# Batch ends of a cross-covariance attention and gated FFN kernel: wide norms, an inverse in four pieces, and two PSUM banks for the folded weights

One Trainium2 chip, one core. The metric is the device time of one execution in microseconds (us). Inputs are random; q, k, v are 4 x 6016 x 256.

## What is computed

```python
qn = q / (norm(q, axis=1) + 1e-6)            # columns of q and k scaled to length 1, per batch
kn = k / (norm(k, axis=1) + 1e-6)
s = kn.transpose(0, 2, 1) @ qn / tau         # 256 x 256 per batch, tau = 1
a = softmax(s, axis=-1)
x = (v @ a).reshape(24064, 256)
gate = 1 / (1 + exp(-(x @ w_gate)))          # w_gate, w_val: 256 x 1536
out = (gate * (x @ w_val)) @ w_out           # w_out: 1536 x 256
```

## The kernel before

PSUM is the memory that TensorE's matmuls write to; a buffer of a PSUM pool is called a bank here. hT is the gated hidden layer, transposed. The softmax matrix is folded into the weights once per batch: G = a @ w_gate and H = a @ w_val, each 256 x 1536. Then v goes straight through G and H. A batch is 12 chunks of 512 tokens (the last has 384), and each chunk is 12 slots, one per 128 columns of the hidden layer. Work for the next batch (its scores, its norms, its softmax, its G and H) is hung into the slots as side work. So three times in a run, at the end of batches 0, 1 and 2, the next batch's attention matrix is finished between the matmuls of the current one. The first batch's is made in a prologue.

```python
psg = pool("psg", 2, space=PSUM)   # gate products
psv = pool("psv", 2, space=PSUM)   # val products
pso = pool("pso", 2, space=PSUM)   # output products
pss = pool("pss", 1, space=PSUM)   # scores of the next batch
psm = pool("psm", 1, space=PSUM)   # norms, row sums, G/H products
# ... 8 buffers in all

def glu(b, ci, f):                 # one slot
    # 2 matmuls into ps_gate, 2 into ps_val (512 columns each)
    nc.scalar.activation(out=g_sb[:, :n], in_=ps_gate[:, :n], func=ACT.Sigmoid)
    nc.vector.tensor_tensor(out=hT[:, f, :n], in0=ps_val[:, :n], in1=g_sb[:, :n], op=ALU.mult)

def norms_mm(b):                   # chunk 9, slot 10: squared norms as one column per 128 channels
    s["n"] = psm.tile([P, 2 * CB], FP32, tag="m", name="ps_n")
    norm_mms(s["n"], s["acc"], TPC, True, True)      # 16 products of one column

def spread_k(b):                   # chunk 10, slot 2: k's inverse norms along the free axis, in fp32
    s["rk"] = pso.tile([P, C], FP32, tag="o", name="ps_rk")
    # ... matmuls of the column, broadcast, with the fp32 identity

# side work of the next batch n at the end of a batch
at(9 * FC + 10, norms_mm, n)
at(9 * FC + 11, norms_sqrt, n)     # ScalarE: a table load, the root, a table load back
at(10 * FC + 1, norms_inv, n)      # VectorE: + 1e-6, reciprocal of 128 x 4
at(10 * FC + 2, spread_k, n)
# ... copy the scores out of PSUM (slot 1), scale them (slot 4), exp (slot 11)
at(11 * FC + 0, sums, n)           # row sums of exp, in psm
for i in range(len(gh_order)):     # 12 G/H pieces, each 2 matmuls of 512 in psm, then an eviction
    at(11 * FC + i, gh, n, i)

# the main loop: in chunks 9 and 10 the output products of the chunk before are not spread
# over the slots, but come as a block of 4 x 12 after slot 11
block = b + 1 < B and ci in (9, 10)
# ...
if prev is not None and block:
    for s in range(TPC):
        out_mms(*prev, s * FC, (s + 1) * FC)   # 12 matmuls into a pso buffer
        flush()                                # VectorE copies it out
```

## Time and profile before

The median was 842.0 us over three runs.

| engine | busy us | share of 837.4 |
|---|---|---|
| TensorE | 816.6 | 98% |
| VectorE | 565.3 | 68% |
| ScalarE | 389.3 | 46% |

Three views carry the argument: TensorE's timeline around a batch end, ScalarE's and VectorE's there, and the groups of instructions by shape. The prediction shows their lines. One reading habit is used all through: on a pipelined TensorE the distance between *starts* says what an instruction cost, and its duration does not. A pair of 512-column matmuls is listed with 0.59, but the next pair starts 0.43 after it. A start that comes later than this is a wait, whether the bracket at the end of the line names one or not. For VectorE it is the same on a smaller scale: an operation of 0.69 lets the next start after 0.61.

This gives four numbers per batch end, each a difference of two starts: the norms (first norm product to the next gate product), the block of output products of chunk 9, chunk 10 (its first gate product to its first output product) and chunk 11 (its first gate product to the first of the next batch). Before, they are 0.40, 5.24, 11.71 and 19.44 us, and the whole from the first norm product to the next batch takes 42.89, the same to 0.01 at all three ends.

### The profile page before, as it was taken

The numbers are of one execution on the slowest core, as the hardware profiler recorded it, in microseconds if no ns is written. First come the engines' busy times: TensorE is split into PE (matmuls) and PEld (weight loads), VectorE is DVE, ScalarE is ACT, GpSimd is POOL, SyncE is SP. The second block draws the span as 40 slices with busy tenths as digits, with TensorE's granted clock in tenths as the row PEclk, the third lists the DMA queues.
The fourth block names the chain that finished last, engine by engine and source line by source line (L and its number), as shares of the span: only waits on it lengthen the run. The fifth ranks groups of instructions, "written<-read, shape, count | busy, mean of one in ns | idle before, by whom it ended". The sixth has DMA issues, their size and how long they took to land.

```text
span 837.4 us, 13986 instructions
## 1 busy us (share of the span) xinstructions
PE 816.6 (98%) x5327; PEld 506.3 (60%) x5338; DVE 565.3 (68%) x976; ACT 389.3 (46%) x639; POOL 83.9 (10%) x161
## 2 busy tenths in 40 slices
PE   5899999999999999999999999999999999999998
PEld 4546666665666666665566666666566565656666
DVE  2477777776667777777656777777766666666664
ACT  3554444446544444444554444444654444444442
POOL 5532100002011100000210020000000000000000
PEclk9899999999999999999999999999999999999999
DMA  9999624227655543223864353223222522322211
GB/s 176 206 206 188 131 51 89 61 51 142 119 102 107 101 108 63 48 51 89 150 136 86 88 117 78 51 76 67 58 48 51 95 51 76 76 48 68 48 35 69
DMA packets 78738, 76.65 MB, mean 92 GB/s; under 512 B 50768, under 2 KB 55632, under 8 KB 78672
## 3 DMA queue, kind: packets, MB, share of 16 engines
q0 software_dynamic: 24208, 39.33, 28.4%
q1 hardware_dynamic: 54464, 36.45, 15.8%
q8 instruction: 41, 0.67, 0.3%
q14 instruction: 25, 0.20, 0.1%
HBM read 78.64 MB, written 24.64 MB: 123 GB/s over the span
## 4 chain that ended last, share of the span: by engine, by line
PE 91%; DMA 3%; DVE 2%; ACT 1%; issue 1%; POOL 0%; ACTq 0%; POOLq 0%
PE ps_o L88 29%; PE ps_gate L88 28%; PE ps_val L88 28%; PE ps_s L88 4%; DMA k_sb<-in_k_dram 3%; PE ps_gh L88 2%; DVE hT L344 1%; ACT g_sb L343 1%; PE ps_rk L88 0%; ACT gh_H L299 0%; DVE out_sb L370 0%; PE ps_n L88 0%; DVE gh_G L301 0%; DVE gh_H L301 0%; DVE x_sb L246 0%
## 5 line engine op out<-in xcount | busy, mean ns | idle before, releaser
L344 DVE TENSOR_TENSOR hT<-ps_val,g_sb 128x512 bf16<-128x512 f32 (+1 forms) x576 | 390.9, 679 | 220.1 <-ACT g_sb L343 216.2
L343 ACT ACTIVATE g_sb<-ps_gate 128x512 bf16<-128x512 f32 (+1 forms) x576 | 338.6, 588 | 400.0 <-PE ps_gate L88 387.6
L88 PE MATMUL ps_val<-vT,gh_H 128*128 128x512 bf16 (+1 forms) x1152 | 338.1, 375 | 0.5
L88 PE MATMUL ps_gate<-vT,gh_G 128*128 128x512 bf16 (+1 forms) x1152 | 337.5, 375 | 0.5
L88 PE MATMUL ps_o<-w_out_sb,hT 128*128 128x256 bf16 x2256 | 326.1, 273 | 0.0
L88 PEld LDWEIGHTS <-hT 128*128 128x128 bf16 x2256 | 220.7, 98 | 124.8
L88 PEld LDWEIGHTS <-gh_H 128*128 128x128 bf16 x1152 | 112.7, 98 | 132.9 <-ACT gh_H L299 1.5
L88 PEld LDWEIGHTS <-gh_G 128*128 128x128 bf16 x1152 | 112.4, 98 | 37.3 <-ACT gh_G L299 0.3
L370 DVE COPY out_sb<-ps_o 128x256 f32<-128x256 f32 x188 | 78.0, 415 | 20.9 <-PE ps_o L88 20.9
L106 POOL DMA_DIRECT2D v_sb<-in_v_dram x48 | 25.5, 531 | 631.3 <-DMA vT<-v_sb 496.3
L88 PE MATMUL ps_s<-k_sb,q_sb 128*128 128x256 bf16 x376 | 72.3, 295 | 12.2 <-DMA k_sb<-in_k_dram 12.2
L88 PEld LDWEIGHTS <-q_sb 128*128 128x128 bf16 x376 | 39.1, 104 | 20.3 <-issue 7.5
L162 DVE TENSOR_TENSOR sq<-q_sb 128x1024 bf16<-128x1024 bf16 (+3 forms) x46 | 30.4, 661 | 25.3 <-PE ps_n L88 19.1
L200 DVE TENSOR_TENSOR acc<-acc,sq 128x1024 bf16<-128x1024 bf16 (+1 forms) x66 | 44.1, 669 | 0.0
L97 POOL DMA_DIRECT2D k_sb<-in_k_dram x49 | 26.9, 549 | 14.5 <-DMA k_sb<-in_k_dram 9.1
L97 POOL DMA_DIRECT2D q_sb<-in_q_dram x49 | 26.8, 548 | 13.7 <-DMA q_sb<-in_q_dram 6.3
L162 DVE TENSOR_TENSOR sq<-k_sb 128x1024 bf16<-128x1024 bf16 (+2 forms) x34 | 22.4, 658 | 0.0
L160 ACT ACTIVATE sq<-k_sb 128x1024 bf16<-128x1024 bf16 (+1 forms) x12 | 12.2, 1021 | 20.1 <-DMA k_sb<-in_k_dram 19.7
L88 PE MATMUL ps_gh<-w_gate,e_sb 128*128 128x512 bf16 x41 | 12.8, 378 | 1.6 <-DVE rrow L274 1.2
L88 PEld LDWEIGHTS <-e_sb 128*128 128x128 bf16 x112 | 9.9, 97 | 6.8 <-issue 3.2
L88 PE MATMUL ps_gh<-w_val,e_sb 128*128 128x512 bf16 x44 | 13.2, 379 | 0.4
L299 ACT ACTIVATE gh_G<-ps_gh,rrow 128x512 bf16<-128x512 f32 x12 | 8.2, 687 | 9.7 <-PE ps_gh L88 5.6
(44 smaller groups left out, 99.7 us busy)
## 6 DMA issues: line engine op xcount, KB each, us to landing
out_dram<-out_sb SPq DMA_DIRECT2D x44, 512.0 KB, 2.9
q_sb<-in_q_dram POOLq DMA_DIRECT2D x44, 256.0 KB, 6.7
k_sb<-in_k_dram POOLq DMA_DIRECT2D x44, 256.0 KB, 7.6
v_sb<-in_v_dram POOLq DMA_DIRECT2D x44, 256.0 KB, 3.9
out_dram<-out_sb SPq DMA_DIRECT2D x4, 384.0 KB, 2.4
w_gate<-in_moe_w_gate_dram POOLq DMA_DIRECT2D x3, 256.0 KB, 7.0
w_val<-in_moe_w_val_dram POOLq DMA_DIRECT2D x3, 256.0 KB, 7.6
w_out_sb<-in_moe_w_out_dram POOLq DMA_DIRECT2D x1, 768.0 KB, 13.0
```

Source lines behind the costliest of these rows:

```text
L88: nc.tensor.matmul(out, lhsT=lhsT, rhs=rhs, start=start, stop=stop, **kw)
L97: nc.gpsimd.dma_start(out=tl[:, :nt, :], in_=rows(src, b)[:, t0 : t0 + nt, :])
L106: nc.gpsimd.dma_start(out=v_sb[:, :nt, :], in_=rows(v, b)[:, t0 : t0 + nt, :])
L160: nc.scalar.activation(out=sq[:, :nt, :], in_=src[:, :nt, :], func=ACT.Square)
L162: engine.tensor_tensor(out=sq[:, :nt, :], in0=src[:, :nt, :], in1=src[:, :nt, :], op=ALU.mult)
L200: nc.vector.tensor_tensor(out=acc[:, :nt, :], in0=acc[:, :nt, :], in1=st[b]["sq", w][:, :nt, :], op=ALU.add)
L299: nc.scalar.activation(out=dst, in_=ps, func=ACT.Copy, scale=r)
L343: nc.scalar.activation(out=g_sb[:, :n], in_=ps_gate[:, :n], func=ACT.Sigmoid)
L344: nc.vector.tensor_tensor(out=hts[b, ci][:, f, :n], in0=ps_val[:, :n], in1=g_sb[:, :n], op=ALU.mult)
L370: nc.vector.tensor_copy(out=out_sb[:, s, :], in_=ps)
```

## The change

The intent: fewer and better placed waits at the batch ends. k's squared norms come out of TensorE already spread over all partitions (a sum over rows by a matrix of ones, 256 columns: the wide norms), so the fp32 spreading falls away. ScalarE takes the root of 256 columns, and VectorE inverts them in four pieces of 64 in four slots. q's norms stay one column per 128 channels, inverted in slot 1. The scores are scaled straight from PSUM, without the copy. The row sums keep slot 0 of chunk 11, the G/H products start one slot later, and they alternate between the bank of the scores, free by then, and the bank of the norms.

```diff
     def norms_mm(b):
-        s["n"] = psm.tile([P, 2 * CB], FP32, tag="m", name="ps_n")
-        norm_mms(s["n"], s["acc"], TPC, True, True)
+        acc_q, acc_k = s["acc"]
+        s["n"] = psm.tile([P, CB], FP32, tag="m", name="ps_n")
+        s["nk"] = pso.tile([P, C], FP32, tag="o", name="ps_nk")
+        for u in range(TPC):
+            mm(s["nk"], ones_bf, acc_k[:, u, :], u == 0, u == TPC - 1)
+        norm_mms(s["n"], (acc_q,), TPC, True, True)
+
+    def wide_sqrt(b):
+        ...
+        nc.scalar.activation(out=s["rk"], in_=s["nk"], func=ACT.Sqrt)
+        nc.scalar.activation(out=s["r"], in_=s["n"], func=ACT.Sqrt)
+
+    def wide_inv(b, piece):
+        ...
+        cols = ds(piece * (C // 4), C // 4)
+        r = s["rk"][:, cols]
+        nc.vector.tensor_scalar(out=r, in0=r, scalar1=1e-6, scalar2=None, op0=ALU.add)
+        nc.vector.reciprocal(r, r)
+
+    def wide_scale(b, j):
+        nc.vector.tensor_tensor(out=s["x"][:, j, :], in0=s["s"][:, j, :], in1=s["rk"], op=ALU.mult)
 ...
-        at(9 * FC + 11, norms_sqrt, n)
+        at(9 * FC + 11, wide_sqrt, n)
         at(10 * FC + 1, norms_inv, n)
-        at(10 * FC + 2, spread_k, n)
+        for i in range(4):
+            at(10 * FC + 2 + i, wide_inv, n, i)
         for j in range(CB):
-            at(10 * FC + 1, copy_s, n, j)
-        at(10 * FC + 4, scale_k, n)
+            at(10 * FC + 6 + j, wide_scale, n, j)
 ...
         for i in range(len(gh_order)):
-            at(11 * FC + i, gh, n, i)
+            at(11 * FC + min(i + 1, FC - 1), gh, n, i, *((pss, "s"), (psm, "m"))[i % 2])
```

More of the change, by code (lines that the diff above doesn't have):

```diff
@@ L205, in norms_mm @@
         s = st[b]
-        s["n"] = psm.tile([P, 2 * CB], FP32, tag="m", name="ps_n")
-        norm_mms(s["n"], s["acc"], TPC, True, True)
+        acc_q, acc_k = s["acc"]
[5 more added lines that the diff above has]
+    def wide_sqrt(b):
+        s = st[b]
+        s["r"] = attp.tile([P, CB], FP32, tag="rq", name="rq")
+        s["rk"] = attp.tile([P, C], FP32, tag="rk", name="rk")
+        nc.scalar.activation(out=s["rk"], in_=s["nk"], func=ACT.Sqrt)
+        nc.scalar.activation(out=s["r"], in_=s["n"], func=ACT.Sqrt)
+    def wide_inv(b, piece):
+        s = st[b]
+        if piece == 0:
+            s["x"] = attp.tile([P, CB, C], FP32, tag="x", name="x_sb")
+        cols = ds(piece * (C // 4), C // 4)
[3 more added lines that the diff above has]
+    def wide_scale(b, j):
+        s = st[b]
+        nc.vector.tensor_tensor(
+            out=s["x"][:, j, :], in0=s["s"][:, j, :], in1=s["rk"], op=ALU.mult
+        )
     def norms_sqrt(b):
```

## The prediction

> **What bounds the kernel now.** I read the page first (engine shares), then TensorE's timeline around the first batch end, then ScalarE's and VectorE's there, then the groups by shape.
>
> The page says TensorE is nearly always busy:
>
> ```profile
> PE 816.6 (98%) x5327; PEld 506.3 (60%) x5338; DVE 565.3 (68%) x976; ACT 389.3 (46%) x639; POOL 83.9 (10%) x161
> ```
>
> A 98% busy TensorE does not say that it never waits, as matmul ends are modelled and overlap. Its timeline shows the waits as gaps between starts. Columns: start, duration, engine, line, operation, count, idle before.
>
> ```profile
> 199.83 0.54 PE L88 MATMUL ps_n<-ones_bf,acc 128*128 128x1 bf16 x16
> 200.23 0.59 PE L88 MATMUL ps_gate<-vT,gh_G 128*128 128x512 bf16 x2
> ...
> 201.09 5.40 PE L88 MATMUL ps_o<-w_out_sb,hT 128*128 128x256 bf16 x48
> 206.33 0.59 PE L88 MATMUL ps_gate<-vT,gh_G 128*128 128x512 bf16 x2
> ...
> 208.49 0.60 PE L88 MATMUL ps_val<-vT,gh_H 128*128 128x512 bf16 x2
> 209.49 0.71 PE L88 MATMUL ps_rk<-ident_f,r 128*128 128x128 f32 x4 [0.41 <-DVE r L217]
> 210.03 0.59 PE L88 MATMUL ps_gate<-vT,gh_G 128*128 128x512 bf16 x2
> ...
> 213.49 0.59 PE L88 MATMUL ps_gate<-vT,gh_G 128*128 128x512 bf16 x2
> 214.16 0.59 PE L88 MATMUL ps_val<-vT,gh_H 128*128 128x512 bf16 x2
> ```
>
> Two matmuls of 512 start every 0.433 us, so a slot of chunks 9 and 10, one gate and one val product, takes 0.866. The 48 output products take 206.33 - 201.09 = 5.24, or 0.109 each. Between 208.49 and 209.49 there is 0.57 too much (0.433 expected); the spreading of k's norms then costs 210.03 - 209.49 = 0.54; the val product at 214.16 is 0.24 late. Together 1.35 us in chunk 10.
>
> Chunk 11, where the G/H products are made:
>
> ```profile
> 224.37 0.24 PE L88 MATMUL ps_r<-ones_bf,e_sb 128*128 128x1 bf16 x4
> 225.01 0.38 PE L88 MATMUL ps_gh<-w_gate,e_sb 128*128 128x512 bf16 x1 [0.40 <-DVE rrow L274]
> ...
> 230.64 0.60 PE L88 MATMUL ps_o<-w_out_sb,hT 128*128 128x256 bf16 x4
> 231.37 0.59 PE L88 MATMUL ps_gh<-w_gate,e_sb 128*128 128x512 bf16 x2
> ```
>
> Four row sums need about 0.10, so the first G/H product is 0.54 late; it waits for the reading of the row sums out of the one bank that both use. The one at 231.37 is 0.29 late (four 0.109 products end at 231.08), and the one at 240.77 the same. The typical slot is 1.52. Sum 1.12.
>
> So one batch end loses 2.47 us to waits and spreading, three of them 7.4 us, 0.9% of the time. This is a ceiling for the gain; batch 0's norms are made in the prologue, which the change leaves alone. The rest is matmul streaming that is not touched.
>
> **What the Trainium skill says.** "TensorE: Matmul & The Clock Gate", section "Back-to-back issue gap": N/2.4 + 2.5 ns for a warm matmul and a floor of about 25 ns for the smallest. The trace agrees: 109 ns at 256, and 16 one-column products in 200.23 - 199.83 = 0.40, or 25 ns each.
>
> "ScalarE: Activation LUTs", section "What ACT_TABLE_LOAD costs": about 1283 ns for a load, 0.833 ns per element for an activation plus a fixed part. The trace has 1283 ns for the loads and, for sigmoid, 597 ns at 512 and 487 ns at 384, or 0.86 ns per element.
>
> "VectorE: DVE Perf Modes", section "Walkthrough: the 8-slice pipeline in each mode", says that Reciprocal is an iterative divide with a repeat count of 8. I read it as some 8 cycles per element, 8.3 ns at that page's 0.96 GHz. The trace has it only at two tiny sizes, in the groups by shape (busy us, mean ns, idle):
>
> ```profile
> L217 DVE RECIPROCAL r<-r 128x4 f32<-128x4 f32 x4 | 0.7, 178 | 0.1
> L275 DVE RECIPROCAL rrow<-rrow 128x2 f32<-128x2 f32 x4 | 0.7, 166 | 0.1
> ```
>
> Two more elements cost 12 ns, so 6 ns each. It is not a streaming one nanosecond, but two points so near together are a weak measure, and this is the number on which the prediction hangs.
>
> **The change, chunk by chunk, per batch end.**
>
> Chunk 9, norms. Removed: 8 one-column products for k, 8 x 0.025 = 0.20. Added: 4 products of 256, 4 x 0.109 = 0.44. Net +0.24.
>
> Chunk 9, a new wait. The wide norms lie in one of the two buffers of the output pool. The first output product of the block takes the other buffer, and the second takes this one; the built program has a wait for ScalarE in front of that second group. ScalarE frees it only after slot 11's sigmoid, a table load and the wide square root:
>
> ```profile
> 200.86 0.60 ACT L343 ACTIVATE g_sb<-ps_gate 128x512 bf16<-128x512 f32 x1 [0.67 <-PE ps_gate L88]
> 201.47 1.28 ACT L212 ACT_TABLE_LOAD   x1
> 202.77 0.17 ACT L212 ACTIVATE r<-ps_n 128x4 f32<-128x4 f32 x1
> ```
>
> Before, nobody waited for that root at once. Now all moves by 0.24, so the root starts at 203.01 and takes 0.17 + 252 x 0.85 ns = 0.385 (estimate from these rows); with 0.06 to TensorE the second group may start at 203.46. It would be due at 201.33 + 12 x 0.109 = 202.64. New wait: +0.82.
>
> Chunk 10, removed: the wait for the inverse, the fp32 spreading, the late val: -1.35. Two PSUM copies of the scores and two scalings become two scalings straight from PSUM. Added on VectorE: four pieces of add and reciprocal over 64 columns. What VectorE's beat leaves for them:
>
> ```profile
> 208.45 0.69 DVE L344 TENSOR_TENSOR hT<-ps_val,g_sb 128x512 bf16<-128x512 f32 x1 [0.17 <-ACT g_sb L343]
> 209.06 0.16 DVE L216 TENSOR_SCALAR r<-r 128x4 f32<-128x4 f32 x1
> 209.25 0.18 DVE L217 RECIPROCAL r<-r 128x4 f32<-128x4 f32 x1
> 209.35 0.72 DVE L240 COPY x_sb<-ps_s 128x256 f32<-128x256 f32 x2
> ```
>
> The next independent operation starts 0.08 to 0.10 before the last one's end, so one hT product occupies 0.61 of the slot's 0.866: 0.25 is free. A piece is an add, 0.22 until the dependent reciprocal may start, and a reciprocal of 0.166 + 62 x 6 ns = 0.54, less 0.08 overlap: 0.68. It overruns the free time by 0.43, four times: 1.70. The small inverse in slot 1 overruns by 0.03, the two scalings (0.33 each) by 0.08 each. VectorE falls behind by 1.89. TensorE feels this soon: there are two val buffers, and val of slot f+2 needs hT of slot f. In the steady beat that hT ends 1.95 us after its slot's start and the val product is due at 2.17; less the passing-on, 0.17 to 0.18 is forgiven. Stall: 1.89 - 0.18 = 1.71. At 8.3 ns per element a piece takes 0.82 and the stall is 2.29; at 1 ns it takes 0.37 and the stall is 0.5. Net in chunk 10: +0.36, +0.94 or -0.85.
>
> Chunk 11: one slot later the row sums' inverse is long ready (-0.54), and with two banks the products no longer wait for the eviction one slot earlier (-0.58): -1.12. Two products share the last slot, on different banks and different evicting engines, and the scores' bank is asked for only 1.3 us after the last product in it has streamed; with the 0.69 eviction done by then, no new wait.
>
> Sum per batch end: 0.24 + 0.82 + 0.36 - 1.12 = +0.30 at 6 ns, +0.88 at 8.3 ns, -0.91 at 1 ns; three times: +0.9, +2.6, -2.7 us.
>
> **The rivals.** (a) The intended gain: no new wait in chunk 9, pieces that fit the slot: 3 x (0.24 - 1.35 - 1.12) = -6.7, 835 us. Against it: the wait stands in the built program, and the root's start is bound by the table load. (b) A gain in chunk 11 with cheap reciprocals: -2.7, about 839; for it, that 12 ns between two sizes may be a coarse clock tick and not a slope; against it, the page and that somebody found it worth cutting the inverse into four. (c) VectorE becomes the bound of chunk 10 and the pieces only spread its overrun: +0.9 to +2.6, 843 to 845. The 0.25 us of room per slot speaks for it. (d) ScalarE or the late VectorE delays the start of the next stage: hardly, the 5.24 us block of output products after each of chunks 9 and 10 lets both catch up.
>
> **Range and chances.** I weigh 6 ns and 8 ns at about 0.4 each and 1 ns at 0.2; the mean is +0.9, and I lean a little to the iterative divide: +1.2 us, 843.2. An error of a fifth of a us in one wait is 0.6 in the whole. Range 839.0 to 845.8. A fall by 2% is 17 us, more than twice the ceiling; a rise by 2% would need 5.6 us more per batch end. So within 2% almost surely: 0.98, and 0.01 on each side.
>
> **What would show it right or wrong.** In the changed kernel's TensorE timeline: the wide norms and small norms take 0.64 rather than 0.40; an idle of some 0.8 before the thirteenth output product of chunk 9's block, released by the square root; no spreading in chunk 10, but val products each about 0.4 late from slot 5 to slot 8; regular 1.52 us slots in chunk 11. The 64-column reciprocal should show 0.54 to 0.68 us. The prediction is wrong if that reciprocal takes about 0.23, if the buffer of the wide norms is not the one that stalls, or if slower VectorE work, hidden so far, appears in the next batch's first chunk.

## The result and the profile after

The changed kernel took 840.88 us (median of 6 runs, 839.51 to 841.5) beside 841.4 before (6 runs, 839.72 to 842.13). The ratio is 0.9995, with a 95% interval from 0.9982 to 1.0008: no difference that the times can show. Ratios here and below are the mean time of one kernel's runs over that of the other's runs of the same rounds, so not quite the ratio of the medians. Executions over 1.5% slower than the fastest of the same kernel are left out of the means.

The profiled executions alone would mislead: the changed kernel's span is 839.2, 1.8 us *longer* than before. The first batch end shows where that comes from: its norms start at 199.83 before and at 201.45 after, 1.62 us later. The first gate product of the run starts at 40.09 before and at 41.71 after, 1.62 later too. So this part lies in the prologue, which the change leaves alone. The pages' rows of granted TensorE clock, in 40 slices of the span, differ in one digit. Before:

```profile
PEclk9899999999999999999999999999999999999999
```

After:

```profile
PEclk9799999999999999999999999999999999999999
```

In the second slice, the end of the prologue, this execution was granted 0.7 and not 0.8 of the clock. TensorE also waits there for k's loads, and no run separates the two. Stages must therefore be compared, not spans. TensorE's timeline after, chunk 9 and a part of chunk 10 (start, duration, engine, line, operation, count, idle before):

```profile
201.45 0.60 PE L88 MATMUL ps_nk<-acc,ones_bf 128*128 128x256 bf16 x4
201.89 0.34 PE L88 MATMUL ps_n<-ones_bf,acc 128*128 128x1 bf16 x8
202.09 0.59 PE L88 MATMUL ps_gate<-vT,gh_G 128*128 128x512 bf16 x2
...
202.95 1.47 PE L88 MATMUL ps_o<-w_out_sb,hT 128*128 128x256 bf16 x12
205.06 4.09 PE L88 MATMUL ps_o<-w_out_sb,hT 128*128 128x256 bf16 x36 [0.64 <-ACT rk L218]
...
214.40 0.59 PE L88 MATMUL ps_gate<-vT,gh_G 128*128 128x512 bf16 x2
215.20 0.59 PE L88 MATMUL ps_val<-vT,gh_H 128*128 128x512 bf16 x2 [0.21 <-DVE hT L372]
```

The norms take 202.09 - 201.45 = 0.64. The thirteenth output product should have started 12 x 0.109 = 1.31 after the first, at 204.26; it started at 205.06, so 0.80 late. The bracket says 0.64, because the page lets the last matmul's pipeline end later, and it names the wide root (rk) as releaser. The val product at 215.20 should have come 0.43 after its gate product and came 0.80 after it. ScalarE's timeline shows the root:

```profile
203.33 1.28 ACT L218 ACT_TABLE_LOAD   x1
204.63 0.38 ACT L218 ACTIVATE rk<-ps_nk 128x256 f32<-128x256 f32 x1
```

It ends at 205.01, and TensorE goes on at 205.06. VectorE in chunk 10:

```profile
212.00 0.69 DVE L372 TENSOR_TENSOR hT<-ps_val,g_sb 128x512 bf16<-128x512 f32 x1
212.60 0.18 DVE L228 TENSOR_SCALAR rk<-rk 128x64 f32<-128x64 f32 x1
212.82 0.55 DVE L229 RECIPROCAL rk<-rk 128x64 f32<-128x64 f32 x1
213.29 0.63 DVE L372 TENSOR_TENSOR hT<-ps_val,g_sb 128x512 bf16<-128x512 f32 x1
213.84 0.18 DVE L228 TENSOR_SCALAR rk<-rk 128x64 f32<-128x64 f32 x1
```

No idle bracket stands on these lines: VectorE sets the beat here, 1.29 us for the first slot with a piece (213.29 - 212.00) where TensorE needs 0.86. In chunk 11 all waits are gone:

```profile
227.13 0.24 PE L88 MATMUL ps_r<-ones_bf,e_sb 128*128 128x1 bf16 x4
...
228.32 0.59 PE L88 MATMUL ps_gh<-w_gate,e_sb 128*128 128x512 bf16 x2
...
229.84 0.59 PE L88 MATMUL ps_gh<-w_gate,e_sb 128*128 128x512 bf16 x2
```

The G/H pairs follow each other at 1.52 us; only the last two stand together in one slot. Set side by side, per batch end:

| stage, us | before | after | difference |
|---|---|---|---|
| norms | 0.40 | 0.64 | +0.24 |
| chunk 9's output block | 5.24 | 6.04 | +0.80 |
| chunk 10 | 11.71 | 11.82 | +0.11 |
| chunk 11 | 19.44 | 18.32 | -1.12 |
| first norm to next batch | 42.89 | 42.92 | +0.03 |

Chunk 9's last slot (0.86) and the block after chunk 10 (5.24), which are in no row, are equal. From one batch end to the next the rest is 158.85 in both (401.57 - 199.83 - 42.89 before, 403.22 - 201.45 - 42.92 after). So the change gives 1.12 and takes back 1.15, three times.

### The profile page after: what moved, and what is told of

It is laid out like the page before. It is cut to its first block, busy times and chain, and to the rows that moved or that the text cites. A ratio compares the mean times of both kernels' runs of the same rounds, so it can differ in the third digit from the quotient of the medians.

```text
span 839.2 us, 13972 instructions
## 1 busy us (share of the span) xinstructions
PE 818.0 (97%) x5314; PEld 506.1 (60%) x5314; DVE 570.1 (68%) x994; ACT 390.6 (47%) x642; POOL 84.1 (10%) x161
## 4 chain that ended last, share of the span: by engine, by line
PE 92%; DMA 3%; DVE 2%; issue 1%; ACT 1%; POOL 0%; POOLq 0%
PE ps_o L88 29%; PE ps_val L88 28%; PE ps_gate L88 28%; PE ps_s L88 4%; DMA k_sb<-in_k_dram 3%; PE ps_gh L88 2%; DVE hT L372 1%; ACT L218 0%; ACT g_sb L371 0%; PE ps_n L88 0%; ACT gh_H L327 0%; DVE rk L228 0%; PE ps_nk L88 0%; POOL q_sb L97 0%; ACT rk L218 0%
## 5 line engine op out<-in xcount | busy, mean ns | idle before, releaser
L327 ACT ACTIVATE gh_H<-ps_gh,rrow 128x512 bf16<-128x512 f32 x12 | 8.3, 688 | 7.2 <-PE ps_gh L88 7.1
```

The costliest lines, as they stand in the source:

```text
L327: nc.scalar.activation(out=dst, in_=ps, func=ACT.Copy, scale=r)
```

## The experiments

The theory after the result is the prediction's: the parts add, the G/H part gains, and the norms part gives it back by two new waits, one on an output buffer and one on VectorE. The rivals: nothing was to be gained in the first place since TensorE streams anyway; a wait that is removed turns up elsewhere; the val products are late for another reason than the length of the reciprocals. All eight kernels ran in five rounds beside the kernel before, in two sets of four: 841.05 before in the first set, 840.56 in the second (medians of 9 runs each). The record names chip 0 for the first set and chip 4 for the second, so ratios are taken within a set.

The stages of all runs, read from the starts in their traces, per batch end (all three ends agree within 0.02). An undisturbed chunk 10 takes 10.36, as two of the experiments show, so "stall" is chunk 10 less 10.36. The expectations were written with 10.39 (12 slots of 0.866), so their stalls are 0.03 smaller. "Worked out" is 1 + 3 x (whole - 42.89)/841.

| run | norms | block 9 | chunk 10 (stall) | chunk 11 | whole | worked out | measured ratio, 95% |
|---|---|---|---|---|---|---|---|
| before | 0.40 | 5.24 | 11.71 (1.35) | 19.44 | 42.89 | 1 | 1 |
| after | 0.64 | 6.04 | 11.82 (1.46) | 18.32 | 42.92 | 1.0001 | 0.9995, 0.9982 to 1.0008 |
| e1 G/H alone | 0.40 | 5.24 | 11.72 (1.36) | 18.32 | 41.78 | 0.9960 | 0.9961, 0.9948 to 0.9974 |
| e2 norms alone | 0.64 | 6.04 | 11.83 (1.47) | 19.44 | 44.05 | 1.0041 | 1.0036, 1.0024 to 1.0049 |
| e3 other bank | 0.64 | 5.24 | 11.82 (1.46) | 18.32 | 42.12 | 0.9973 | 0.9961, 0.9948 to 0.9975 |
| e4 inverse in block | 0.64 | 6.04 | 10.36 (0) | 18.32 | 41.46 | 0.9949 | 0.9938, 0.9925 to 0.9950 |
| e5 one piece | 0.64 | 6.04 | 11.89 (1.53) | 18.32 | 42.99 | 1.0004 | 1.0009, 0.9996 to 1.0023 |
| e6 every other slot | 0.64 | 6.04 | 10.90 (0.54) | 18.32 | 42.01 | 0.9969 | 0.9964, 0.9950 to 0.9977 |
| e7 e3 and e4 | 0.64 | 5.24 | 10.36 (0) | 18.32 | 40.66 | 0.9920 | 0.9911, 0.9897 to 0.9925 |
| e8 no reciprocal | 0.64 | 6.04 | 10.61 (0.25) | 18.32 | 41.71 | 0.9958 | 0.9957, 0.9943 to 0.9970 |

Every interval holds the number worked out from the trace. The stages repeat to 0.01 us while whole executions of one kernel scatter by 1 to 2.6 us.

**e1: the G/H part alone.** The kernel before, with the last line of the change only.

```diff
-            at(11 * FC + i, gh, n, i)
+            at(11 * FC + min(i + 1, FC - 1), gh, n, i, *((pss, "s"), (psm, "m"))[i % 2])
```

> The kernel before with only the G/H part of the change (two banks, one slot later). Main theory (the parts add up; the gain of chunk 11 is real and is paid back elsewhere): chunk 11 falls from 19.44 to 18.32 us at each of the three batch ends, chunks 9 and 10 stay as before, so 3 x 1.12 = 3.4 us less than before, ratio 0.996. Rival (TensorE was streaming anyway and the waits in chunk 11 cost nothing, or they come back at the start of the next batch): ratio 1.000.

837.86 us (5 runs). Chunk 11 fell to 18.32 and nothing else moved. The rival that TensorE had nothing to gain falls: the gain of this part is real and whole. The edit makes two changes at once, the later slot and the second bank; no run separates what each of them gives.

**e2: the norms part alone.** The changed kernel with that hunk taken back.

```diff
-            at(11 * FC + min(i + 1, FC - 1), gh, n, i, *((pss, "s"), (psm, "m"))[i % 2])
+            at(11 * FC + i, gh, n, i)
```

> The changed kernel with the G/H part taken back, so only the wide norms and the inverse in four pieces are left. Main theory: chunk 9 gains 0.24 for the products and 0.80 for the wait on the output buffer, chunk 10 is 0.1 longer than before (1.43 of stall in place of 1.32), chunk 11 stays at 19.44: 3 x 1.15 = 3.4 us more than before, ratio 1.004. Rival (the norms part is neutral, the G/H part too): ratio 1.000.

844.2 us (5 runs), slower than before with an interval clear of 1. The two parts are -1.11 and +1.16 per batch end: together +0.05, and the whole change has +0.03. They add, and the unchanged time of the whole is a gain and a loss of the same size.

**e3: the wide norms in the bank of the small ones.** One tile of 258 columns in the psm bank; the first product of q's norms is issued with start=False, so that it does not start the bank anew.

```diff
-        s["n"] = psm.tile([P, CB], FP32, tag="m", name="ps_n")
-        s["nk"] = pso.tile([P, C], FP32, tag="o", name="ps_nk")
+        ps = psm.tile([P, C + CB], FP32, tag="m", name="ps_n")
+        s["nk"] = ps[:, :C]
+        s["n"] = ps[:, C : C + CB]
 ...
-        norm_mms(s["n"], (acc_q,), TPC, True, True)
+        norm_mms(s["n"], (acc_q,), TPC, False, True)
```

> The changed kernel with the wide norms put into the bank of the small norms, so that the output pool is not used. Main theory: the idle of 0.80 before the thirteenth output product of chunk 9's block goes and nothing takes its place: chunk 10 keeps its 1.43 of stall; 3 x 0.80 = 2.4 us less than the changed kernel, 2.3 less than before, ratio 0.997. Rival (the wait was ScalarE's table switch, which then holds up something later, such as the first sigmoid of chunk 10): the idle turns up elsewhere and the ratio stays at 0.9995.

837.82 us (5 runs), result correct. TensorE's timeline has the block in one piece again, 5.24 until the next gate product:

```profile
202.85 5.40 PE L88 MATMUL ps_o<-w_out_sb,hT 128*128 128x256 bf16 x48
208.09 0.59 PE L88 MATMUL ps_gate<-vT,gh_G 128*128 128x512 bf16 x2
```

Chunk 10 kept its stall of 1.46. So the 0.80 was the wait for a buffer and went without a trace; ScalarE's table load and root take as long as ever (1.28 and 0.38), but nobody stands behind them. What each of the two adds to the wait no run separates.

**e4: the inverse in the block.** The four pieces leave chunk 10 and stand in chunk 9's block, one after each copy of an output tile.

```diff
-        for i in range(4):
-            at(10 * FC + 2 + i, wide_inv, n, i)
 ...
                     flush()
+                    if ci == 9:
+                        wide_inv(b + 1, s)
```

> The changed kernel with the four pieces of the inverse moved into chunk 9's block of output products, one after each copy of an output tile, where VectorE sat idle 0.89 us of every 1.31. Main theory (the late val products in chunk 10 come from the pieces that do not fit the 0.25 us of room): chunk 10's stall falls from 1.43 to under 0.15, the wait of 0.80 in chunk 9 stays; 3 x 1.3 = 3.9 us less than the changed kernel, ratio to before 0.9955. Rival (the val products are late because the scaling reads the scores from PSUM, or for ScalarE): stall stays near 1.4, ratio 0.9995.

835.4 us (5 runs). VectorE's timeline in the block:

```profile
206.47 0.42 DVE L398 COPY out_sb<-ps_o 128x256 f32<-128x256 f32 x1 [0.20 <-PE ps_o L88]
206.81 0.18 DVE L228 TENSOR_SCALAR rk<-rk 128x64 f32<-128x64 f32 x1
207.03 0.55 DVE L229 RECIPROCAL rk<-rk 128x64 f32<-128x64 f32 x1
207.78 0.43 DVE L398 COPY out_sb<-ps_o 128x256 f32<-128x256 f32 x1 [0.20 <-PE ps_o L88]
```

The same add and reciprocal of 0.18 and 0.55, in an idle time of which 0.20 is still left before the next copy. Chunk 10's stall is zero with the scalings from PSUM still in slots 6 and 7 and ScalarE's work unchanged, so neither of these makes a stall by itself. (Behind the pieces the scalings still count: in the changed kernel the last two late val products, 0.07 each, stand in slots 9 and 10.) The gain was a little more than expected since I had left a remainder of 0.15 for the scalings, and they fit into the time that is forgiven.

**e5: one piece instead of four.** All 256 columns in slot 2.

```diff
-        cols = ds(piece * (C // 4), C // 4)
+        cols = ds(0, C)
 ...
-        for i in range(4):
-            at(10 * FC + 2 + i, wide_inv, n, i)
+        at(10 * FC + 2, wide_inv, n, 0)
```

> The changed kernel with the inverse of all 256 columns in one piece in slot 2 of chunk 10, not four of 64 over four slots. Theory of the room (what counts is VectorE's total work beyond 0.25 us a slot): an add of about 0.3 and a reciprocal of 0.17 + 254 x 6.2 ns = 1.74 overrun by some 1.7 once, and the scalings fit later: stall 1.4 to 1.6 against 1.43, time within 0.6 us of the changed kernel. Rival (cutting is what keeps the stall small, a long operation holds hT for two slots and stalls more): stall over 2.0, 2 us or more above the changed kernel.

841.46 us (5 runs); stall 1.53 against 1.46. Cutting the inverse into four saved 0.07. The groups by shape (busy us, mean ns, idle):

```profile
L229 DVE RECIPROCAL rk<-rk 128x256 f32<-128x256 f32 x3 | 5.3, 1752 | 0.1
L228 DVE TENSOR_SCALAR rk<-rk 128x256 f32<-128x256 f32 x3 | 0.8, 283 | 0.0
```

What counts is the sum of VectorE's work beyond its room in these slots, the 0.25 of the prediction, and four neighbouring slots that are each too full are hardly better than one.

**e6: pieces in every other slot.** Slots 2, 4, 6, 8, and the scalings in 9 and 10.

```diff
-            at(10 * FC + 2 + i, wide_inv, n, i)
+            at(10 * FC + 2 + 2 * i, wide_inv, n, i)
 ...
-            at(10 * FC + 6 + j, wide_scale, n, j)
+            at(10 * FC + 9 + j, wide_scale, n, j)
```

> The changed kernel with the four pieces in slots 2, 4, 6, 8 and the scalings in slots 9 and 10. Theory of the room: after each piece VectorE gets a slot in which it works off 0.25, and 0.18 is forgiven each time, so each piece stalls TensorE by about 0.2 instead of 0.37: stall 0.7 to 1.0 against 1.43, 3 x 0.55 = 1.6 us less than the changed kernel, ratio to before 0.9975. Rival (each piece costs its overrun wherever it stands): stall 1.4, no change.

837.38 us (5 runs); stall 0.54, so the direction is the theory's and the rival falls, but the expected 0.7 to 1.0 was too much. The cause of the miss is the same as in the prediction (below): the hT product behind a reciprocal is shorter than I took it to be.

**e7: both repairs.** e3 and e4 in one kernel.

> The changed kernel with the wide norms in the small norms' bank and the inverse in chunk 9's block: the version that the theory points to. If the parts add: per batch end +0.24 for the norms, no wait in chunk 9, stall in chunk 10 under 0.15 instead of 1.32, -1.12 in chunk 11: -2.1, three times -6.3 us against before, ratio 0.9925. If the two waits hide each other, only the larger of the two gains comes: ratio 0.995.

833.26 us (median of 4 runs, 832.82 to 833.86), result correct. The two waits do not hide each other: 42.89 - 40.66 = 2.23 us less per batch end, and the ratio is 0.9911. It is the fastest version here, and it takes 2.23 of the 2.47 us that the prediction named as ceiling; what is left beyond plain streaming at a batch end are the norms (0.64) and the row sums.

**e8: no reciprocal.** Wrong (relative error 0.79): the same number of operations, with a cheap one in place of the reciprocal.

```diff
-        nc.vector.reciprocal(r, r)
+        nc.vector.tensor_scalar(out=r, in0=r, scalar1=1.0, scalar2=None, op0=ALU.mult)
```

> Wrong result on purpose: the changed kernel with each 64-column reciprocal replaced by a multiplication by 1.0 of the same columns, so the count of operations stays and only the 6 ns per element go. Theory (the reciprocal's time per element makes the stall): an operation of 0.18 in place of 0.55, the pieces overrun by some 0.07 each, stall 0.2 to 0.4 against 1.43: 3 x 1.1 = 3.3 us less than the changed kernel, ratio to before 0.9965. Rival (the number of small operations, not their length, makes it): stall over 1.0, ratio 0.999.

837.32 us (5 runs); stall 0.25. In the groups by shape:

```profile
L229 DVE TENSOR_SCALAR rk<-rk 128x64 f32<-128x64 f32 x12 | 2.3, 195 | 0.4
```

195 ns in place of 553 takes 1.21 of the 1.46. It is the reciprocals' length, not the count of small operations. VectorE's timeline shows one thing more:

```profile
211.37 0.20 DVE L229 TENSOR_SCALAR rk<-rk 128x64 f32<-128x64 f32 x1
211.48 0.68 DVE L372 TENSOR_TENSOR hT<-ps_val,g_sb 128x512 bf16<-128x512 f32 x1
```

The hT product behind the short operation takes 0.68, where behind the reciprocal it took 0.63. Four operations shorter by 0.358 are 1.43; four products longer by 0.06 are 0.24; the difference, 1.19, is close to the 1.21.

## Why the prediction was right

It said 843.2 us, range 839.0 to 845.8, and within 2% with a chance of 0.98; the time was 840.88. The time by itself confirms little: with a ceiling of 0.9% the result was within 2% almost whatever the mechanism, and rival (b)'s 839 lies in the range too. The steps are the test, and by these the prediction was right in mechanism. Per batch end:

- *The ceiling.* 2.47 us per batch end to waits and spreading. Confirmed: e7, with neither old nor new waits, is 2.23 below before, and the norms cost 0.24 more there: 2.47.
- *Norms, +0.24.* Measured +0.24.
- *The new wait on the output buffer, +0.82.* Measured +0.80, with the root of 0.38 that was estimated as 0.385, and e3 shows that it is that buffer.
- *Chunk 10, +0.36 at 6 ns per element.* Measured +0.11. The mechanism was right (e4, e8) and a term was mis-sized: VectorE's fall behind of 1.89, and so the stall of 1.71, which was 1.46. The reciprocal was right: 553 ns against 0.54. The term that failed is the 0.61 that an hT product was said to occupy in each slot. In the trace after, 213.29 to 213.84 is 0.55: the hT product right behind a 64-column reciprocal is 0.63 long and not 0.69. The beat of the first slot with a piece was 1.29, as predicted, and of the next three 1.23. Four slots have such a product, 4 x 0.06 = 0.24, and 1.71 - 0.24 = 1.47 against 1.46. Standing behind some operation is not enough: behind one of 195 ns it is 0.68 (e8). Why it is shorter behind the reciprocal no run here shows. The same 0.06 makes e6 better than expected: 0.8 expected less 4 x 0.06 is 0.56, against 0.54. The val products were late from slot 5 on, as the prediction said: by 0.23, then three times 0.37, and then twice 0.07.
- *Chunk 11, -1.12.* Measured -1.12, and e1 shows it alone; its split into 0.54 and 0.58 is argued and not tested. The scores' bank has more time than the prediction's 1.3 us: the last G/H pair in it starts at 243.50, so it has streamed by 243.93, and the next scores start at 245.67, 1.74 later.
- *Sum, +0.30 at 6 ns.* Measured +0.03. The lean to the slower divide (8.3 ns), which raised the estimate from +0.9 to +1.2 us, was wrong: it is 6.2 ns.
- *Rival (a), the intended gain,* was wrong in chunk 9 for the reasons given against it, and in chunk 10 because the pieces do not fit the slot. With both repaired, e7 is at -2.23 per batch end, which is rival (a)'s sum. *Rival (b), a cheap reciprocal,* is what e8 builds: its stall is 0.25 where 0.5 was estimated, mostly because a piece takes 0.32 there (211.16 to 211.48 in e8) and not 0.37, four times. *Rival (c)* is what happened. *Rival (d)* did not: the block after chunk 10 and the rest of the batch are equal to 0.01.

Of the distance between 843.2 and 840.88, the prediction's +1.2 against the +0.1 that the traces show (3 x 0.03) is 1.1 us. The other part is the median before, 842.0 when predicted and 841.4 in the result, and scatter.

## What to carry to other kernels

A change that frees a stage must be followed into the buffers that it borrows: a tile put into a double buffer that is about to be used hard makes the next user wait for the slowest reader, here a ScalarE root behind a table load. When an engine keeps a beat with little room, spreading long work over neighbouring slots gives nothing; put it where the engine is idle (here a block of matmuls with one copy per 1.31 us), or leave empty slots between. If a change leaves the time as it was, run its parts alone before calling them neutral: here they were -0.4% and +0.4%, and with the loss repaired the same idea gave -0.9%.

## What the Trainium skill lacked or had wrong

- "VectorE: DVE Perf Modes" gives Reciprocal a repeat count of 8 and no time per element. The runs show 166 ns for 2 columns, 553 for 64 and 1752 for 256 (fp32 in SBUF): 6.2 ns per element between each two of them, about 6 cycles at the page's 0.96 GHz, not the 8 that the prediction read out of it.
- No page has an operation being shorter behind a reciprocal: the 128x512 hT product takes 0.63 us behind a 64-column reciprocal, with the next operation 0.55 after its start, and 0.68 or 0.69 in the other places shown here, with the next one 0.60 or 0.61 after. In e4 and e7 a product that starts 0.50 after a reciprocal's start, and not 0.47, takes 0.69 again: it had to wait for its sigmoid there.
- "ScalarE: Activation LUTs", section "What ACT_TABLE_LOAD costs", counts about 1380 ns of drain on top of the load of 1283, 2.66 us for a switch. Here a load starts 0.01 after the sigmoid's end, at 203.33, and the root starts at 204.63: a switch cost 1.30 in all.
- No page has the price of borrowing a buffer from a pool in use; it is 0.80 us of TensorE here, the time that the second group of the block waits for the root that reads the borrowed bank (e3: without the loan it is 0).
- The formula that the prediction cites from "TensorE: Matmul & The Clock Gate", section "Back-to-back issue gap", stands there for an isolated matmul; for a sustained stream of 512 columns the section gives about 131 ns. The stream here runs at 216 ns (0.433 us for two), as the formula has it, and not at 131.
